# A Winograd-style convolution kernel: fewer matmuls on zeros, loads in another order, one product moved

## The chip, the cores and the metric

The kernel runs on one core of a Trainium2 chip. The core has a matmul engine (PE, with its weight loads shown as PEld), a vector engine (DVE), a scalar engine (ACT), a general engine (POOL) and a sync engine (SP) that here only issues DMAs. ACT and POOL can issue DMAs too. Sixteen DMA engines serve all of them. The metric is the device time of one execution in microseconds; it is a little longer than the span in the profile, which runs from the first to the last instruction.

## The reference

A one-dimensional convolution with three taps over two sequences, then a batch normalisation with given statistics, then SiLU. B = 2 sequences of S = 2048 positions, C = 1024 channels in and out, bf16 inputs:

```python
xp = jnp.pad(x, ((0, 0), (P, P), (0, 0)))
y = sum(jnp.einsum('bsc,cd->bsd', xp[:, k:k + S, :], w[k]) for k in range(K))
inv_std = 1.0 / jnp.sqrt(var + 1e-5)
y = (y - mean) * (g * inv_std) + b
return _silu(y)
```

## The kernel before

**The method.** Six neighbouring outputs are made from eight inputs by eight products (numbered 0 to 7, one for each evaluation point) instead of eighteen. There are 342 groups of six outputs in each sequence.

**Input transform.** For each sequence `bi` and each of the 8 channel tiles `ct`, a load (`load_x`, 512 KB) brings 16 frames of 128 positions. One matmul per frame with the fixed matrix `rm` (168 columns, line 292) makes the transformed input in PSUM; six or four such matmuls share a pair of PSUM banks and are one job (`Jobs.do`). ACT or DVE copies the pair to the bf16 tile `T_sb` (lines 306 and 308). The last 6 groups of a sequence come from a short block `xl` (`load_small`, 8 matmuls of 48 columns, line 281). In the text, x(b,ct) is the tile `ct` of sequence b. Tiles of x have six buffers, so the seventh load waits until PE has used the first.

**Weight transform.** For each output tile `dc` POOL, with help from ACT (line 144) and DVE (line 160), makes six transformed weight tiles `u` from the three taps (lines 146 to 167). Products 0 and 7 use taps 0 and 2 as they are. Before that POOL computes the normalisation's scale and shift from the parameters `prm` (lines 236 to 243).

**Units.** A unit is one output tile of one sequence: 8 products of 8 accumulating matmuls of 342 columns each. The first unit is a class of its own (`First`, line 462), the other fourteen and the two halves of the last one use `Unit.run` (line 336). ACT and DVE combine the products and ACT applies SiLU. In `Unit.run` the products come in the order 1, 3, 2, 4, 5, 6. Product 5 goes to bank 2 of the unit's four, ACT copies it out, and product 6 is then added in the same bank; so product 6 waits for that copy. In later units, work of the unit before stands between 5 and 6 (`behind(5)`); in the second unit there is none.

**What sets the order.** The kernel writes the order of every engine's instructions out by hand, as the program is built. For the first part it keeps a small plan: `clock` holds a planned time for each engine and for the DMA stream, `landed` the planned landing of each load, and each job is given to the PSUM bank pair that is planned to be free first and to ACT or DVE, whichever is planned to end first. While sequence 0 is transformed, `keep_busy` puts matmuls on a tile of zeros (line 101) wherever the plan sees PE waiting. They write to the bank that the next job will use. Then the main loop takes turns between sequence 1's jobs and the first unit's products, whichever the plan has ready. From the second unit on no plan is used.

**Queues.** SP issues nearly all loads, in program order: short block 0, the first halves of x(0,0) and x(0,1), x(0,2), taps 0 and 2, x(0,3) to x(0,5), tap 1, x(0,6), x(0,7), short block 1, and sequence 1's tiles. ACT issues `rm` and the two second halves. POOL issues `prm`. Loads on SP's and ACT's queues take one of eight landing semaphores in turn, so a load waits until the load eight places before it has landed.

Of the kernel before, what the change touches and what calls it, by code (L numbers as in the profile page):

```python
# [9 lines left out]
FP32 = mybir.dt.float32  # L10
BF16 = mybir.dt.bfloat16
ENG = mybir.EngineType

P = 128
# [2 lines left out]
WT = 21  # L17
XBUFS = 6
WARM_AT = 7000.0
LROWS = 48  # L20
NTILES = 342
NBP = 384
# [3 lines left out]
def kernel(  # L26
# [9 lines left out]
    nc = tc.nc  # L36
    B, CT, _, NF, _ = x.shape
    DC = w.shape[0]
# [5 lines left out]
    consts = ctx.enter_context(tc.tile_pool(name="consts", bufs=1))  # L44
# [17 lines left out]
    ps = pspool.tile([P, 8, 512], FP32, name="ps")  # L62
# [3 lines left out]
    rm = consts.tile([P, NJ, WT], BF16, name="rm")  # L66
    nc.scalar.dma_start(out=rm, in_=rm_in)
    prm = consts.tile([P, 4, DC], BF16, name="prm")
    nc.gpsimd.dma_start(out=prm, in_=prm_in)

    zeros = consts.tile([P, 384], BF16, name="zeros")
    nc.vector.memset(zeros, 0.0)
    dummy = consts.tile([P, 2], FP32, name="dummy")
    nc.vector.memset(dummy, 0.0)


    clock = {"pe": 1150.0, "act": 3700.0, "dve": 1500.0, "pool": 7000.0, "dma": 2300.0}
    cost = {"act": (0.833, 170.0), "dve": (1.042, 155.0), "pool": (2.0, 80.0)}

    def ends(e, size, ready):  # L80
# [2 lines left out]
    def busy(e, size, ready=None):  # L83
        clock[e] = ends(e, size, clock["pe"] + 250.0 if ready is None else ready)
        return clock[e] + 100.0
# [8 lines left out]
    def matmuls(cols):  # L94
        clock["pe"] += cols / (2.34 if clock["pe"] > WARM_AT else 1.18)

    def keep_busy(until, bank):

        n = 384 if clock["pe"] > WARM_AT else 192
        while clock["pe"] + 150.0 < until:  # L100
            nc.tensor.matmul(ps[:, bank, 0:n], lhsT=zeros[:, 0:P], rhs=zeros[:, 0:n], start=True, stop=True)  # L101
            matmuls(n)

    xt, xt_at, raw, raw_at = {}, {}, {}, {}
    small, small_at = {}, {}
# [1 line left out]
    def load_small(bi):  # L107
        t = xlpool.tile([P, CT * P], BF16, name="xl")
        nc.sync.dma_start(out=t[0:LROWS], in_=xl[bi])  # L109
        small[bi], small_at[bi] = t, landed(LROWS * CT * P * 2)  # L110

    def load_x(bi, ct, parts=1):
        t = xpool.tile([P, NF, P], BF16, name="xw")
        xt[bi, ct], xt_at[bi, ct] = t, []
        step = NF // parts
        for q in range(parts):
            s = slice(q * step, (q + 1) * step)
            (nc.scalar if q else nc.sync).dma_start(out=t[:, s], in_=x[bi, ct, :, s])
            at = landed(P * step * P * 2)
            xt_at[bi, ct] += [at] * step  # L120

    def load_w(dc, taps):
        if dc not in raw:
            raw[dc] = wpools[dc // 2 % 2].tile([P, 3, CT, P], BF16, name=f"wch{dc // 2 % 2}")
        if len(taps) == 3:
            nc.sync.dma_start(out=raw[dc], in_=w[dc])
        else:
            for k in taps:
                nc.sync.dma_start(out=raw[dc][:, k], in_=w[dc, :, k])
        for k in taps:  # L130
            raw_at[dc, k] = landed(P * CT * P * 2)
# [117 lines left out]
    class Jobs:  # L249


        def __init__(self, bi):
            self.bi = bi
            self.todo = [(None, 0, 0)] + [
                (ct, f, min(6, NF - f)) for ct in range(CT) for f in range(0, NF, 6)
            ]

        def __bool__(self):
            return bool(self.todo)
# [60 lines left out]
    class Unit:  # L320
# [57 lines left out]
                (first, lambda: self.first(between)),  # L378
            ][::1 if first >= min(last, 5) else -1]

        def run(self, between, also=(), prepare=None, later=False):
            def behind(n):
                for at, f in also:
                    if at == n:
                        f()

            b0, b1, b2, b3 = self.bank
            sl = slice(self.lo, self.hi)
            sd = dpool.tile([P, 4, NB], FP32, name="sd")[:, 0:3:2, sl]
            t0 = dpool.tile([P, 2, NB], FP32, name="t0")[:, :, sl]  # L390
            t2 = dpool.tile([P, 2, NB], FP32, name="t2")[:, :, sl]
            self.y23 = t1 = ypool2.tile([P, 2, NB], FP32, name="t1")[:, :, sl]
            self.product(3, 1, False, between)
            pa = self.copy(3)
            behind(1)
            self.product(0, 3, False, between)
            pb = self.copy(0, by=4.0)
            behind(2)
            self.product(3, 2, True, between)
            self.copy(3, dst=sd[:, 0])  # L400
            self.combine(sd[:, 1], pa, 2.0, b3, ALU.subtract)
            behind(3)
            self.product(0, 4, True, between)
            behind(4)
            self.combine(b1, b0, -2.0, pb)
            for t, a in ((t0, -0.0125), (t1, -0.05), (t2, -0.2)):
                self.combine(t, self.low, a, sd)
            idle(dve_work)
            if prepare:
                prepare_w(prepare)  # L410
            self.product(2, 5, False, between)
            pc = self.copy(2)
            behind(5)
            self.product(2, 6, True, between)
            self.combine(b3, b2, -0.5, pc)
            self.combine(self.low, self.high, -1.6, t0)
            self.combine(t1, self.high, -0.4, t1)
            self.combine(self.high, self.high, -0.1, t2)
            behind(6)
            if prepare and not later:  # L420
                idle(act_work)
                idle(dve_work)
# [123 lines left out]

    load_small(0)
    load_x(0, 0, 2)  # L550
    load_x(0, 1, 2)
    nc.scalar.activation(dummy[:, 1:2], dummy[:, 0:1], ACT.Silu)
    for ct in range(2, CT):
        load_x(0, ct)
        if ct == 2:
            load_w(0, (0, 2))
        if ct == 5:
            load_w(0, (1,))
    load_small(1)
    for ct in range(CT):  # L560
        load_x(1, ct)
# [19 lines left out]
    while jobs[1] or unit.todo[0][0] != 6:  # L581
        if len(second) == 3 and len(jobs[1].todo) < 6:
            second.pop(0)()
        at = jobs[1].place()[1] if jobs[1] else None
        if at is not None and (not unit.todo or at <= max(clock["pe"], unit.at())):
            jobs[1].do()
        else:
            unit.do()
# [6 lines left out]
    for i, (dc, bi) in enumerate(seq[1:-1], 1):  # L595
        unit = Unit(dc, bi, i % 2 * 4)
        also = prev.rest(quiet)
        if i == 1:
            also = [(1, second[0]), (4, second[1])] + also
        if i == 2:  # L600
            also = prev.rest(quiet, 4, 5)
        if i == 3:
            also = also + [(1, lambda: idle(act_work)), (1, lambda: idle(dve_work))]
        if i == len(seq) - 2:
            also = prev.rest(quiet, 4, 5)
        unit.run(
            quiet, also,
            2 if i == 2 else dc + 2 if bi == 1 and 0 < dc < DC - 2 else None, i == 2,
        )
        if bi == 0 and dc + 3 < DC:  # L610
            load_w(dc + 3, (0, 1, 2))
        prev.store(nc.sync)
        prev = unit

    dc, bi = seq[-1]
# [87 lines left out]
```

## Time and profile before

| | |
|---|---|
| time, median of 3 runs | 185.26 us (185.02 to 186.8) |
| time of the profiled execution | 185.67 us |
| its span | 183.9 us |
| PE, DVE, ACT, POOL busy | 176.6, 149.1, 110.0, 141.6 us |
| DMA | 24.60 MB, mean 134 GB/s |
| granted TensorE clock | 1.000 |

A page of the profile names an instruction by engine and line, then what it writes and reads. The chain of waits is followed back from the last instruction: each piece is what the next one had to wait for. Matmuls overlap, so a group's busy time includes one drain; the pace is the distance between starts. The matmuls' rate is best read from that pace, since the row of the granted clock shows full speed in every slice.

### The profile page before, as it was taken

How to read it: one execution, taken by the hardware profiler on the slowest of the kernel's cores; microseconds unless marked ns; L12 is line 12 of the kernel's file. 1: busy time of each engine (PE TensorE's matmuls, PEld its weight loads, DVE VectorE, ACT ScalarE, POOL GpSimd, SP SyncE). 2: the span in 40 equal slices, each digit the busy share in tenths (PEclk: the TensorE clock that was granted, in tenths of full speed). 3: DMA queues.
4: the chain of work that ended last, by engine and by line, in shares of the span. 5: the costliest groups of instructions: out<-in, count | busy, mean ns of one | idle time of the engine just before them, and what ended most of it. 6: DMA issues, size and time to landing. Idle time of an engine off the chain costs nothing.

```text
span 183.9 us, 3516 instructions
## 1 busy us (share of the span) xinstructions
PE 176.6 (96%) x1385; PEld 127.1 (69%) x1385; DVE 149.1 (81%) x192; ACT 110.0 (60%) x174; POOL 141.6 (77%) x78
## 2 busy tenths in 40 slices
PE   6999999898999999999999999999999999999992
PEld 4988888765666666666666666666666666668891
DVE  1169768699977999999997899789978999766690
ACT  3688997945665565456554745474547454563763
POOL 3599999989996779999999999999999776000000
PEclk9999999999999999999999999999999999999999
DMA  5999991080307030363036303620202020113042
GB/s 177 400 418 371 411 384 68 16 303 29 130 0 267 36 128 4 76 225 128 4 76 223 128 4 56 243 112 18 110 22 96 32 94 40 79 49 129 3 176 86
DMA packets 7089, 24.60 MB, mean 134 GB/s; under 512 B 944, under 2 KB 1344, under 8 KB 7072
## 3 DMA queue, kind: packets, MB, share of 16 engines
q1 hardware_dynamic: 6464, 23.73, 35.2%
q10 hardware_dynamic: 576, 0.63, 1.0%
q8 instruction: 11, 0.18, 0.4%
q14 instruction: 6, 0.05, 0.1%
q0 software_dynamic: 32, 0.01, 0.1%
HBM read 14.93 MB, written 9.44 MB: 132 GB/s over the span
## 4 chain that ended last, share of the span: by engine, by line
PE 89%; DVE 4%; ACT 3%; DMA 2%; issue 1%; SPq 0%; DVEq 0%; ACTq 0%
PE ps L336 73%; PE ps L292 10%; PE ps L462 4%; DMA xw<-in_x_dram 2%; DVE ps L352 2%; PE ps L101 1%; DVE T_sb L308 1%; ACT T_sb L306 1%; DVE t L352 1%; ACT yh L357 1%; ACT w1x L144 1%; ACT pc L345 0%; SPq L109 0%; DVEq L692 0%; PE ps L281 0%
## 5 line engine op out<-in xcount | busy, mean ns | idle before, releaser
L336 PE MATMUL ps<-T_sb,u 128*128 128x342 bf16 (+2 forms) x768 | 109.8, 298 | 0.5 <-ACT pc L345 0.5
L336 PEld LDWEIGHTS <-u 128*128 128x128 bf16 x768 | 72.5, 97 | 33.4 <-issue 0.7
L167 POOL TENSOR_TENSOR u<-e,w1x 128x1024 bf16<-128x1024 f32 x32 | 69.3, 2193 | 7.1 <-DVE e L160 6.4
L336 PE MATMUL ps<-T_sb,wch 128*128 128x342 bf16 (+2 forms) x256 | 39.8, 299 | 0.2 <-DVE ps L352 0.2
L167 POOL TENSOR_TENSOR u<-e,wch 128x1024 bf16<-128x1024 f32 x16 | 37.6, 2369 | 0.6
L352 DVE SCALAR_TENSOR_TENSOR t<-ps,sd 128x684 f32<-128x684 f32 (+2 forms) x49 | 37.5, 819 | 0.6
L357 ACT ACTIVATE yT<-ps,beta,scale 128x342 bf16<-128x342 f32 (+1 forms) x42 | 29.2, 727 | 10.9 <-PE ps L336 10.9
L345 ACT COPY pc<-ps 128x342 f32<-128x342 f32 (+2 forms) x32 | 13.6, 426 | 30.6 <-PE ps L336 28.8
L336 PEld LDWEIGHTS <-wch 128*128 128x128 bf16 x256 | 24.2, 97 | 11.1 <-issue 0.5
L308 DVE CAST T_sb<-ps 128x1008 bf16<-128x1008 f32 (+2 forms) x21 | 20.8, 1011 | 13.4 <-PE ps L292 10.2
L306 ACT CAST T_sb<-ps 128x1008 bf16<-128x1008 f32 (+1 forms) x29 | 25.6, 928 | 5.6 <-PE ps L292 5.5
L352 DVE SCALAR_TENSOR_TENSOR ps<-ps,t 128x684 f32<-128x684 f32 (+2 forms) x32 | 26.5, 829 | 0.5
L292 PE MATMUL ps<-rm,xw 128*128 128x168 bf16 x256 | 24.7, 250 | 1.2 <-ACT T_sb L306 0.7
L160 DVE SCALAR_TENSOR_TENSOR e<-wch 128x1024 f32<-128x1024 bf16 x12 | 25.7, 2141 | 0.0
L292 PEld LDWEIGHTS <-xw 128*128 128x128 bf16 x256 | 21.8, 105 | 4.4 <-issue 1.5
L352 DVE SCALAR_TENSOR_TENSOR ps<-ps,pc 128x342 f32<-128x342 f32 (+2 forms) x34 | 16.9, 496 | 8.4 <-PE ps L336 5.9
L154 POOL TENSOR_TENSOR e<-wch 128x1024 f32<-128x1024 bf16 x8 | 19.0, 2370 | 1.0 <-DMA wch<-in_w_dram 1.0
L357 ACT ACTIVATE yT<-t,beta,scale 128x684 bf16<-128x684 f32 x15 | 14.4, 958 | 0.0
L352 DVE SCALAR_TENSOR_TENSOR t<-ps,t 128x684 f32<-128x684 f32 (+2 forms) x17 | 13.9, 817 | 0.0
L352 DVE SCALAR_TENSOR_TENSOR sd<-pc,ps 128x342 f32<-128x342 f32 (+2 forms) x17 | 8.2, 483 | 6.1 <-ACT sd L345 6.1
L345 ACT COPY sd<-ps 128x342 f32<-128x342 f32 (+2 forms) x16 | 6.8, 428 | 10.4 <-PE ps L336 9.7
L347 ACT ACTIVATE pc<-ps 128x342 f32<-128x342 f32 (+2 forms) x16 | 7.0, 438 | 9.2 <-PE ps L336 6.9
(41 smaller groups left out, 69.1 us busy)
## 6 DMA issues: line engine op xcount, KB each, us to landing
out_dram<-yT SPq DMA_DIRECT2D x15, 576.0 KB, 2.7
xw<-in_x_dram SPq DMA_DIRECT2D x14, 512.0 KB, 6.7
wch<-in_w_dram SPq DMA_DIRECT2D x7, 768.0 KB, 5.4
wch<-in_w_dram SPq DMA_DIRECT2D x3, 256.0 KB, 6.1
xw<-in_x_dram ACTq DMA_DIRECT2D x2, 256.0 KB, 4.6
xw<-in_x_dram SPq DMA_DIRECT2D x2, 256.0 KB, 4.5
out_dram<-yh SPq DMA_DIRECT2D x1, 256.0 KB, 3.7
out_dram<-yh SPq DMA_DIRECT2D x2, 128.0 KB, 2.1
```

Source lines behind the costliest of these rows:

```text
L154: nc.gpsimd.tensor_tensor(sums[dc, q], a, b, op=ALU.add)
L160: nc.vector.scalar_tensor_tensor(out=e, in0=f, scalar=4.0, in1=h, op0=ALU.mult, op1=ALU.add)
L167: nc.gpsimd.tensor_tensor(wts[dc, q][:, i], sums[dc, q], o, op=(ALU.add, ALU.subtract)[i])
L292: nc.tensor.matmul(src[:, q // per, q % per], lhsT=xt[self.bi, ct][:, f + q], rhs=rm, start=True, stop=True)
L306: nc.scalar.copy(dst, src)
L308: nc.vector.tensor_copy(dst, src)
L336: nc.tensor.matmul(self.bank[q], lhsT=lhsT, rhs=T_sb[self.bi][:, ct, j, nsl], start=not add and ct == 0, stop=ct == CT - 1, skip_group_che ...
L345: nc.scalar.copy(dst, self.bank[q])
L347: nc.scalar.mul(dst, self.bank[q], by)
L352: nc.vector.scalar_tensor_tensor(out=out, in0=in0, scalar=scalar, in1=in1, op0=ALU.mult, op1=op1)
L357: nc.scalar.activation(self.yT[:, rows, self.y0:self.y0 + self.hi - self.lo], src, ACT.Silu, bias=beta[:, dc:dc + 1], scale=scale[:, dc:dc ...
L462: nc.tensor.matmul(self.bank[q], lhsT=lhsT, rhs=T_sb[self.bi][:, ct, j, :], start=not add and ct == 0, stop=ct == CT - 1, skip_group_check ...
```

## The change

Zeros: the tile of zeros becomes fp32 with 256 columns, three fp32 matmuls on it are issued ahead of everything, and `keep_busy` works (on the same bytes, read as bf16) only where the plan sees a longer wait: over 200 ns before a planned 9 us, over 900 ns after. In the built program 25 matmuls on zeros become three fp32 ones and five of 192 columns; none of 384 columns are left.

Loads: x(0,0) and x(0,1) come first and the short block third on SP's queue; tap 1 comes behind all of sequence 0's tiles (sequence 1 in the change's own words, which count from one). The parameters go from POOL's queue to ACT's, behind the second halves of x(0,0) and x(0,1).

Jobs: each sequence's short block becomes the seventh job instead of the first. The plan also books 0.85 us plus overhead on ACT when one of the second tile's weight steps is put on ACT. In the new order of PE, sequence 0's tiles 2 to 7 and the first 12 matmuls of x(1,0) follow each other with nothing between, and the first unit's products begin after that.

Second unit: product 5 and the copy behind it come ahead of product 4 (`early`).

```diff
+FILL = 9000.0
@@
-    nc.gpsimd.dma_start(out=prm, in_=prm_in)
-
-    zeros = consts.tile([P, 384], BF16, name="zeros")
+
+    zeros = consts.tile([P, 256], FP32, name="zeros")
     nc.vector.memset(zeros, 0.0)
+    for _ in range(3):
+        nc.tensor.matmul(ps[:, 3, 0:256], lhsT=zeros[:, 0:P], rhs=zeros, start=True, stop=True)
@@
-    clock = {"pe": 1150.0, "act": 3700.0, "dve": 1500.0, "pool": 7000.0, "dma": 2300.0}
+    clock = {"pe": 4150.0, "act": 3700.0, "dve": 1500.0, "pool": 7000.0, "dma": 2300.0}
@@ def keep_busy(until, bank):
-        n = 384 if clock["pe"] > WARM_AT else 192
-        while clock["pe"] + 150.0 < until:
-            nc.tensor.matmul(ps[:, bank, 0:n], lhsT=zeros[:, 0:P], rhs=zeros[:, 0:n], start=True, stop=True)
-            matmuls(n)
+        z = zeros.bitcast(BF16)
+        n, gap, left = (192, 200.0, 100.0) if clock["pe"] < FILL else (384, 900.0, 600.0)
+        if clock["pe"] + gap < until:
+            while clock["pe"] + left < until:
+                nc.tensor.matmul(ps[:, bank, 0:n], lhsT=z[:, 0:P], rhs=z[:, 0:n], start=True, stop=True)
+                matmuls(n)
@@ class Jobs
-            self.todo = [(None, 0, 0)] + [
-                (ct, f, min(6, NF - f)) for ct in range(CT) for f in range(0, NF, 6)
-            ]
+            self.todo = [(ct, f, min(6, NF - f)) for ct in range(CT) for f in range(0, NF, 6)]
+            self.todo.insert(6, (None, 0, 0))
@@ Unit.run(..., early=False)
             self.combine(sd[:, 1], pa, 2.0, b3, ALU.subtract)
             behind(3)
+            if early:
+                self.product(2, 5, False, between)
+                pc = self.copy(2)
             self.product(0, 4, True, between)
             behind(4)
@@
-            self.product(2, 5, False, between)
-            pc = self.copy(2)
+            if not early:
+                self.product(2, 5, False, between)
+                pc = self.copy(2)
             behind(5)
@@
-    load_small(0)
     load_x(0, 0, 2)
     load_x(0, 1, 2)
+    load_small(0)
+    nc.scalar.dma_start(out=prm, in_=prm_in)
     nc.scalar.activation(dummy[:, 1:2], dummy[:, 0:1], ACT.Silu)
     for ct in range(2, CT):
         load_x(0, ct)
         if ct == 2:
             load_w(0, (0, 2))
-        if ct == 5:
-            load_w(0, (1,))
+    load_w(0, (1,))
     load_small(1)
@@
             second.pop(0)()
+            busy("act", CT * P, 0.0)
```

In the call of `unit.run`, `early` is true for the second unit alone (`i == 1`).

More of the change, by code (lines that the diff above doesn't have):

```diff
@@ L379, in rest, with run @@
             ][::1 if first >= min(last, 5) else -1]
-        def run(self, between, also=(), prepare=None, later=False):
+        def run(self, between, also=(), prepare=None, later=False, early=False):
             def behind(n):
@@ L607 @@
             quiet, also,
-            2 if i == 2 else dc + 2 if bi == 1 and 0 < dc < DC - 2 else None, i == 2,
+            2 if i == 2 else dc + 2 if bi == 1 and 0 < dc < DC - 2 else None, i == 2, i == 1,
         )
```

## The prediction

> **What bounds the kernel now.** I read the page first: one core, granted clock full in every slice, PE busy.
>
> ```profile
> span 183.9 us, 3516 instructions
> PE 176.6 (96%) x1385; PEld 127.1 (69%) x1385; DVE 149.1 (81%) x192; ACT 110.0 (60%) x174; POOL 141.6 (77%) x78
> ```
>
> PE bounds the average, so the chain of waits was next (start, length, what, count).
>
> ```profile
> 1.17 3.77 DMA xw<-in_x_dram
> ...
> 4.98 4.68 PE ps L292 x32
> ...
> 10.66 0.48 PE ps L101 x2
> ...
> 11.44 0.65 PE ps L101 x4
> 12.09 0.88 PE ps L292 x12
> ...
> 25.21 1.01 ACT T_sb L306
> ...
> 40.59 4.66 PE ps L336 x32
> 45.25 0.02 issue
> 45.27 0.45 ACT pc L345
> 45.73 0.04 issue
> 45.77 128.81 PE ps L336 x904
> ```
>
> From 45.77 to 174.6 PE never waits; behind that comes a tail that the change leaves alone. All that can move lies before 45.77. There the first 32 input-transform matmuls (L292) take 146 ns each and later ones 73 (12 in 0.88), and matmuls on zeros (L101) stand in the chain among useful work. Third, the same time as stretches (length, then busy time by engine, granted clock, DMA share, GB/s):
>
> ```profile
> 4.98:9.64 4.66, 4.66 (x34) 4.66 (x35) 0.86 (x1) 3.26 (x4) 2.94 (x7) 1.00 1.04 404
> 9.64:19.30 9.66, 9.41 (x108) 7.98 (x106) 8.10 (x8) 8.54 (x11) 9.36 (x7) 1.00 1.03 397
> 19.30:40.43 21.13, 20.43 (x210) 16.60 (x210) 15.84 (x20) 17.07 (x23) 21.04 (x10) 1.00 0.62 227
> 45.07:45.77 0.70, 0.17 (x3) 0.00 (x0) 0.67 (x1) 0.50 (x2) 0.70 (x2) 1.00 0.00 0
> ```
>
> Up to 19.3 us, where sequence 0's 128 transform matmuls end, the DMA engines are full at about 400 GB/s. Last, SP's timeline and the transfers issued around 11.5 us, for the first tile of sequence 1, x(1,0):
>
> ```profile
> 11.47 12.32 SPq L118 DMA_DIRECT2D xw<-in_x_dram x8
> ```
> ```profile
> xw<-in_x_dram SPq DMA_DIRECT2D x1, 512.0 KB, 7.6
> ```
>
> So x(1,0) lands at 11.47 + 7.6 = 19.1. Its first matmul is at 19.65: PE trails the loads by only 0.5 us here.
>
> **Zeros, and what they hide.** Eleven 384-column zeros go, at 163 ns each (0.65 / 4): 1.8 us of PE. Five of 192 columns stay, 0.4 us at that rate per column. This does not reach the end in full. In the new order sequence 0's 128 matmuls and the first 12 of x(1,0) run on end, and x(1,0) cannot come much earlier: the bytes ahead of its last one are the same in both orders (tap 1's 262 KB passes x(0,6) and x(0,7), not x(1,0)). These are nine x tiles of 524 KB, three weight taps of 262, two short blocks of 98 and 51 of parameters, 5.75 MB. At 241 GB/s over 1 to 5 us and 400 after, they are read by 17.0; landing takes until 19.1. I take 19.1. PE then waits for it instead of working on zeros.
>
> From x(1,0) on, PE needs 128 x 73 ns for sequence 1, 64 products of the first unit (`First`) and 8 of the second at 145 ns (4.66 / 32): 9.3 + 9.3 + 1.2 = 19.8 us, whatever the order. Before, this ran from 19.65 to 40.43, 20.8 us, so 1.0 was lost; two waits for a PSUM bank, 25.9 to 26.3 and 34.05 to 34.76, are nearly all of it. The second stands behind ACT's 1.06 us w1x (L144) in the middle of the copies; the change books that time in the plan. After, PE starts at 19.15 and also has sequence 1's short block behind x(1,0), 8 matmuls in 0.3 us. I walked the new order down, job by job: a job of 6 (or 4) matmuls starts when PE is free, its tile has landed and the copy out of its bank pair has ended; its copy starts 0.28 us after its last matmul or when its engine is free, with the trace's pitch (ACT 0.90 us for 1008 columns, 0.61 for 672; DVE 1.17 and 0.82). Over the old order this gives 40.4, as the trace has. Over the new one sequence 0 keeps up with its loads (last tile taken at 16.7, last matmul at 17.8), PE waits until 19.15, and later there are two bank waits, 0.24 and 0.20, both at x(1,3). So 19.15 + 19.8 + 0.3 + 0.45 = 39.7, against 40.43: **0.75 us gained.** Walked with x(1,0) at 18.2 the gain is 1.65, at 19.7 it is 0.15.
>
> **fp32 zeros at the start.** The trace has no fp32 matmul. From below: 192 bf16 columns go every 0.16 us (11 in 1.94, the last one's drain in it), so 256 columns in one pass 0.21, three 0.64. From above: ACT's 1.0 us for a copy of 1008 fp32 columns, for each, 3.0 (the plan, which starts PE's clock at 4150 instead of 1150 ns, books as much). PE starts at 1.15 (the memset of 0.22 us is a third longer); x(0,0) lands at 4.9, and about 4.3 with the short block's 98 KB no longer ahead of it on SP's queue. So 3.2 us are free, and the price is nothing at both ends. Were they 0.8 us too long, sequence 0 would begin 0.8 late and still end before 19.15. The Trainium skill ("FP8 and Floating Point Precision", TensorE Precision Notes) says a true fp32 matmul makes four passes; by that, an estimate of 0.85 each, 2.6 in all, also hidden. What they may bring is an earlier full rate. The trace has PE working from 1.11 us and halving its matmul time only at about 9.6, after pauses at 3.0 and 4.4. The Trainium skill ("TensorE: Matmul & The Clock Gate", Part 1) has the array at full rate after one busy window of some 3.4 us; the trace took longer. By the rule the new start would be fast from 6 instead of 9.6, 24 matmuls x 70 ns = 1.7 us. By my walk that is worth nothing, since PE then waits for x(1,0) so much longer. A full rate that came only at 11.3, 7 us behind x(0,0) instead of 4.7, would cost 0.45 of the gain; I keep that for the range.
>
> **Loads that move.** Each hardware-queue load waits for the landing of the one eight places before. The parameters join this ring on ACT's queue, so SP's w and x issues slip by 0.8 to 1.4 us at 2.6 to 6 us; transfers stand 6.7 us in the queue (median), which covers it. If cover failed, x(1,0) would slip as much. Tap 1 lands about 0.7 behind x(0,7) (17.5 before), so near 17.5; POOL wants it at 18.1. POOL's timeline (start, length, instruction, idle time before it and what ended that):
>
> ```profile
> 5.34 0.20 POOL L238 TENSOR_SCALAR sc<-prm 128x8 f32<-128x8 bf16 x1 [2.50 <-DMA prm<-in_prm_dram]
> ...
> 9.38 2.12 POOL L154 TENSOR_TENSOR e<-wch 128x1024 f32<-128x1024 bf16 x1 [0.97 <-DMA wch<-in_w_dram]
> ```
>
> POOL's own issue of the parameters (0.76 us) goes, at no gain, since POOL then waits 2.50 for them. On ACT's queue they follow x(0,1)'s second half (issued 1.65, landing 7.0). POOL's scale chain (5.34 to 8.41) starts near 7.1, and the POOL work queued behind it slips 0.8 us, 9.38 to 10.2. Its tightest customer is the third unit's fifth product at 52.7, whose weights were ready at 49.6: 3.1 us of slack, 1.7 after the gain. 0.6 of the slip vanishes in POOL's own wait for w1x at 41.05. Nothing; if prm lands after 8.5 it bites one for one. ACT issues it in 0.45 us before its table load, which now ends at 3.9; the first copy is at 5.4.
>
> **Product 5 ahead of product 4.** At 45.07 PE waits 0.70 us for ACT to copy the second unit's bank 2 (0.45 at 45.27) before product 6 may be added there. Now product 4, 8 x 145 = 1.16 us, stands between. The copy needs 0.35 + 0.45: hidden, **0.70 us gained**, if ACT is free. It is: the copy now goes ahead of the second w1x, which slips to end by 44.8, and POOL wants it at 45.2. DVE's combine behind product 4 stood at 44.55, after a queue of the first unit's work; now product 4 ends at 39.7 + 4 x 1.16 = 44.3, and it stands at 44.5. So DVE still leaves that bank at 48.87, and PE, which added the next product there at 51.57, comes at 50.1: free, with 1.2 left.
>
> **Sum.** 0.75 + 0.70 = 1.45 off the span, 183.9 to 182.45. The profiled execution took 185.67, 1.77 more than its span; the median of the runs is 185.26. On that: **183.8**.
>
> **Rivals.**
> *The loads land earlier* (0.20). The reading is done by 17.0 and the landing 2.1 later; if that lag is one slow DMA engine and it does not recur, x(1,0) at 18.2 gives 1.65 + 0.70, **182.9**. Against: all later tiles lag alike.
> *The product moved brings nothing* (0.17): ACT still has sequence 1's copies or w1x in front, and the wait only moves. 0.75 remains: **184.5**. Against: ACT idles 0.75 to 0.9 us before each copy there.
> *The clock falls* (0.10). PE now idles some 0.5 us at 16.2 and 1.3 at 17.8, where zeros stood. If the half rate returns as at the start, PE works 4.66 us at half rate (4.98 to 9.64) and loses 2.3: 1.45 gained becomes 0.85 lost, **186.1**; twice, 188.4. It decides once such pauses count. For it: with 0.32 and 0.54 us of idling ahead of 4.98 the rate stayed half. Against: in the tail PE is busy only 5.5 of 9.3 us and its last matmuls still run 55 ns apart for 128 columns, full rate. The Trainium skill (same page, "HAM oscillation") has the clock fall only behind pauses above some 3.4 us; by that it stays.
>
> **Numbers.** Forecast 0.53, the rivals as given. The range, 182.8 to 185.4, takes in the early landing and the moved product that brings nothing, and leaves out most of the fallen clock and little else. One per cent, about what a measurement tells from no change, is 1.85 us: 183.4 and 187.1. Faster: the early landing, and the lower edge of the forecast, 0.26; slower, half the fallen clock and mishaps of the queues that I did not see, 0.07; the rest 0.67.
>
> **What would show it.** Right: no L101 between 9 and 40 us; a PE wait for x(1,0) just before 19.1; the second unit's matmuls (L340) unbroken from 39.7 to the tail. Wrong: x(1,0)'s first matmul away from 19.15; transform matmuls at 146 ns after 12 us; a PE wait for ACT pc near 44; POOL's first e behind 11.

## The result, and the profile after

The changed kernel takes 185.11 us in the median (184.75 to 185.66), the kernel before, timed beside it, 185.56 (185.02 to 187.23): a ratio of 0.9965, 95% interval 0.9948 to 0.9982. The forecast was 183.8, and 1.45 us of gain; 0.45 came. The 183.8 had also been counted from 185.26, the median of three runs; its twenty runs here give 185.56, so 0.3 of the miss in the time itself is that starting point. The profiled execution took 185.10, 2.1 more than its span.

The page of the changed kernel, its span and the busy time of each engine:

```profile
span 183.0 us, 3476 instructions
PE 175.1 (96%) x1371; PEld 125.1 (68%) x1371; DVE 152.1 (83%) x192; ACT 108.8 (59%) x174; POOL 141.6 (77%) x77
```

PE does 1.5 us less, DVE 3.0 more with the same 192 instructions. That is the first hint: nothing was added to DVE, so its instructions must take longer. The chain of waits (start, length, what, count):

```profile
1.16 4.47 DMA xw<-in_x_dram
...
8.49 0.57 PE ps L106 x5
...
10.25 8.71 DMA xw<-in_x_dram
19.00 1.04 PE ps L296 x12
...
36.66 1.67 DVE sd L356
...
49.55 0.80 DVE ps L356
50.39 4.82 PE ps L340 x32
...
58.70 1.86 DVE e L165
...
78.88 0.80 DVE ps L356
79.71 93.97 PE ps L340 x664
```

Before, PE ran unbroken from 45.77. Now the chain leaves PE twice more, at 50.39 and 79.71, both times for DVE's combine (L356). Between them it runs through DVE instructions of 1.67 and 1.86 us. The wait for ACT's copy at 45 us is gone. PE's waits by what ended them (total, times, longest):

```profile
PE ps L296 <- DMA xw<-in_x_dram: 2.1, 3, 1.3
...
PE ps L340 <- DVE ps L356: 0.4, 2, 0.2
```

These count idle time alone; from the start of one matmul to the start of the next, less the usual 145 ns, PE loses 0.32 and 0.30 at the two places.

The start as stretches (length, then busy time by engine with counts, granted clock, DMA share, GB/s): the first is the one shown of before, the other two are the wait for x(1,0), and what follows up to the second unit's unbroken run.

```profile
4.98:9.64 4.66, 4.24 (x51) 3.77 (x49) 2.53 (x3) 3.72 (x5) 1.30 (x2) 1.00 1.05 375
17.50:19.00 1.50, 0.23 (x4) 0.02 (x2) 1.50 (x2) 0.94 (x1) 1.42 (x2) 1.00 1.03 412
19.00:39.61 20.61, 20.48 (x208) 16.49 (x209) 15.88 (x19) 15.82 (x22) 20.53 (x11) 1.00 0.63 246
```

From 4.98 to 9.64 PE starts 51 matmuls instead of 34 but the loads bring 375 GB/s instead of 404. Then PE stands 1.5 us from start to start before x(1,0), as forecast, and needs 20.61 us from there to 39.61. SP's issue of x(1,0) (and x(1,1)), and the landing time of the first:

```profile
10.25 2.14 SPq L123 DMA_DIRECT2D xw<-in_x_dram  x2
```
```profile
xw<-in_x_dram SPq DMA_DIRECT2D x1, 512.0 KB, 8.7
```

It is issued 1.2 us earlier than before and lands at 18.95, 0.15 earlier. Last, POOL, whose chain starts with the parameters:

```profile
8.26 0.20 POOL L243 TENSOR_SCALAR sc<-prm 128x8 f32<-128x8 bf16 x1 [6.70 <-DMA prm<-in_prm_dram]
...
11.37 2.12 POOL L159 TENSOR_TENSOR e<-wch 128x1024 f32<-128x1024 bf16 x1
```

The first e stands at 11.37, not at the 10.2 of the forecast, and behind the 11 that it named as a sign of being wrong.

The two profiled executions can be added up at PE's last full-size matmul before the tail, which starts at 173.52 before and 172.63 after; the tail is 10.38 in both. The second unit's run starts 0.81 earlier (39.61 for 40.42); the wait of 0.70 at 45 us is gone; a wait of 0.32 at 50.4 and one of 0.30 at 79.7 are new. 0.81 + 0.70 - 0.32 - 0.30 = 0.89, and 173.52 - 172.63 is 0.89. That is twice the gain of the medians. The span of 183.0 is among the three shortest of the kernel's twenty executions, whose median span is 183.3; for the kernel before, the profiled span is 183.9 and the median of the executions timed beside the experiments 183.7. So the experiments ask why those two waits came, and whether the 0.81 of this one execution stands for the others.

### The profile page after: what moved, and what is told of

Same layout as the page of the kernel before. It is cut to its first block, busy times and chain, and to the rows that moved or that the text cites. A ratio compares the mean times of both kernels' runs of the same rounds, so it can differ in the third digit from the quotient of the medians.

```text
span 183.0 us, 3476 instructions
## 1 busy us (share of the span) xinstructions
PE 175.1 (96%) x1371; PEld 125.1 (68%) x1371; DVE 152.1 (83%) x192; ACT 108.8 (59%) x174; POOL 141.6 (77%) x77
## 4 chain that ended last, share of the span: by engine, by line
PE 62%; DVE 24%; DMA 7%; issue 2%; ACT 2%; DVEq 0%; ACTq 0%
PE ps L340 54%; DMA xw<-in_x_dram 7%; DVE ps L356 7%; DVE t L356 6%; PE ps L296 5%; DVE e L165 5%; PE ps L470 2%; DVE T_sb L312 2%; DVE sd L356 2%; DVE f L356 2%; ACT T_sb L310 1%; ACT yh L361 1%; PE ps L106 0%; ACTq L68 0%; DVEq L701 0%
## 5 line engine op out<-in xcount | busy, mean ns | idle before, releaser
L172 POOL TENSOR_TENSOR u<-e,wch 128x1024 bf16<-128x1024 f32 x16 | 38.8, 2439 | 0.5
L356 DVE SCALAR_TENSOR_TENSOR t<-ps,sd 128x684 f32<-128x684 f32 (+2 forms) x49 | 37.5, 819 | 0.6
L312 DVE CAST T_sb<-ps 128x1008 bf16<-128x1008 f32 (+2 forms) x22 | 22.6, 1066 | 11.7 <-PE ps L296 11.6
L310 ACT CAST T_sb<-ps 128x1008 bf16<-128x1008 f32 (+1 forms) x28 | 24.1, 892 | 5.5 <-PE ps L296 5.1
L356 DVE SCALAR_TENSOR_TENSOR ps<-ps,t 128x684 f32<-128x684 f32 (+2 forms) x32 | 26.5, 829 | 0.5
L165 DVE SCALAR_TENSOR_TENSOR e<-wch 128x1024 f32<-128x1024 bf16 x12 | 26.8, 2237 | 0.0
L296 PE MATMUL ps<-rm,xw 128*128 128x168 bf16 x256 | 23.4, 243 | 2.6 <-DMA xw<-in_x_dram 2.1
L296 PEld LDWEIGHTS <-xw 128*128 128x128 bf16 x256 | 20.2, 100 | 6.0 <-DMA xw<-in_x_dram 3.5
L356 DVE SCALAR_TENSOR_TENSOR ps<-ps,pc 128x342 f32<-128x342 f32 (+2 forms) x34 | 16.8, 495 | 8.5 <-PE ps L340 6.1
L356 DVE SCALAR_TENSOR_TENSOR t<-ps,t 128x684 f32<-128x684 f32 (+2 forms) x17 | 13.9, 817 | 0.0
L356 DVE SCALAR_TENSOR_TENSOR sd<-pc,ps 128x342 f32<-128x342 f32 (+2 forms) x17 | 8.2, 483 | 4.5 <-ACT sd L349 4.4
```

The lines of the kernel that those rows point to most:

```text
L165: nc.vector.scalar_tensor_tensor(out=e, in0=f, scalar=4.0, in1=h, op0=ALU.mult, op1=ALU.add)
L172: nc.gpsimd.tensor_tensor(wts[dc, q][:, i], sums[dc, q], o, op=(ALU.add, ALU.subtract)[i])
L296: nc.tensor.matmul(src[:, q // per, q % per], lhsT=xt[self.bi, ct][:, f + q], rhs=rm, start=True, stop=True)
L310: nc.scalar.copy(dst, src)
L312: nc.vector.tensor_copy(dst, src)
L356: nc.vector.scalar_tensor_tensor(out=out, in0=in0, scalar=scalar, in1=in1, op0=ALU.mult, op1=op1)
```

## The experiments

Seven kernels (e1 to e7) undo or single out parts of the change, e8 is the changed kernel again, and seven more (e9 to e15) test what these left open. Each was timed beside the kernel before on the same chip (medians there 185.43 to 185.56); the profiled numbers are of one execution each. "Wait at 50" and "at 80" are what PE loses there, beyond the 145 ns from one matmul to the next.

| run | median us (runs) | ratio to before, 95% | x(1,0) landed | 2nd unit's run from | DVE sd<-sd,kept, ns | wait at 45 / 50 / 80, us |
|---|---|---|---|---|---|---|
| before | 185.56 (20) | 1 | 19.10 | 40.42 | 674 | 0.70 / 0 / 0 |
| after | 185.11 (20) | 0.9965 (0.9948 to 0.9982) | 18.96 | 39.61 | 1669 | 0 / 0.32 / 0.30 |
| e1 | 185.25 (12) | 0.9983 (0.9950 to 1.0015) | 18.92 | 40.14 | 2487 | 0 / 1.41 / 0 |
| e2 | 185.60 (12) | 1.0012 (0.9983 to 1.0042) | 19.61 | 40.27 | 1764 | 0.70 / 0 / 0 |
| e3 | 185.10 (12) | 0.9968 (0.9936 to 1.0000) | 19.69 | 40.35 | 1300 | 0 / 0.32 / 0 |
| e4 | 186.12 (12) | 1.0025 (0.9990 to 1.0061) | 20.91 | 41.57 | 1274 | 0 / 0.33 / 0 |
| e5 | 185.00 (12) | 0.9972 (0.9957 to 0.9988) | 18.40 | 39.51 | 2029 | 0 / 0.66 / 0.34 |
| e6 | 185.11 (12) | 0.9975 (0.9954 to 0.9996) | 18.93 | 39.59 | 1835 | 0 / 0.47 / 0.33 |
| e7 | 185.54 (12) | 0.9998 (0.9982 to 1.0014) | 19.45 | 40.49 | none | 0 / 0.32 / 0 |
| e9 | 185.12 (12) | 0.9968 (0.9950 to 0.9986) | 19.53 | 40.20 | 1593 | 0 / 0.23 / 0.32 |
| e10 | 184.75 (12) | 0.9950 (0.9927 to 0.9972) | 19.23 | 39.90 | 1332 | 0 / 0 / 0 |
| e11 | 185.13 (12) | 0.9983 (0.9957 to 1.0009) | 18.19 | 41.49 | 2396 | 0.70 / 0 / 0 |
| e12 | 183.92 (6) | 0.9901 (0.9873 to 0.9930) | 17.80 | 38.91 | 798 | 0 / 0 / 0 |
| e13 | 184.24 (8) | 0.9937 (0.9916 to 0.9959) | 17.74 | 39.56 | 2257 | 0 / 0.89 / 0 |
| e14 | 184.67 (6) | 0.9952 (0.9935 to 0.9970) | 18.98 | 40.21 | 829 | 0 / 0 / 0 |
| e15 | 184.11 (6) | 0.9929 (0.9905 to 0.9952) | 18.05 | 39.55 | 515 | 0 / 0 / 0 |

**e1: the kernel before with the moved product alone.**

```diff
+            if early:
+                self.product(2, 5, False, between)
+                pc = self.copy(2)
             self.product(0, 4, True, between)
...
-            self.product(2, 5, False, between)
-            pc = self.copy(2)
+            if not early:
+                self.product(2, 5, False, between)
+                pc = self.copy(2)
```

> The kernel before with product 5 ahead of product 4 in the second unit and nothing else. Theory (VectorE's chain of combines and weight sums between 36 and 80 us caps what PE can gain, because those of its instructions that read two SBUF tiles wait until GpSimd's running instruction ends): PE's wait of 0.70 us at 45.1 goes, VectorE leaves bank 0 at about 48.9 while PE comes at 50.9, the first weight sum of VectorE (line 160, near 58.7) still meets an idle GpSimd and takes 1.2 us, and the chain keeps its lead at 79: the whole 0.7 us reaches the end, span about 183.2 where the kernel before has 183.9, ratio about 0.996. Rival (the moved product only moves the wait, or the gain is lost in PE's own stream): span 183.9, ratio 1.000.

The wait at 45 us goes and the median falls by 0.3, not by 0.7; the interval of its ratio takes in no change. DVE's timeline in e1 (start, length, instruction), and the chain's last long piece:

```profile
37.48 2.49 DVE L352 SCALAR_TENSOR_TENSOR sd<-sd,kept 128x342 f32<-128x342 f32 x1
...
51.08 0.87 DVE L352 SCALAR_TENSOR_TENSOR ps<-ps,t 128x684 f32<-128x684 f32 x1
```
```profile
52.00 122.99 PE ps L336 x864
```

PE now waits at 52.00 for the combine that ends at 51.95. One DVE instruction of the first unit took 2.49 us in this execution, where the kernel before shows 0.67 and the same kind of instruction on 342 columns elsewhere 0.5.

**e2: the changed kernel with the old order of products**, so zeros and loads alone.

```diff
-            2 if i == 2 else dc + 2 if bi == 1 and 0 < dc < DC - 2 else None, i == 2, i == 1,
+            2 if i == 2 else dc + 2 if bi == 1 and 0 < dc < DC - 2 else None, i == 2, False,
```

> The changed kernel with the second unit's products in the old order. Theory of VectorE's chain: PE again waits 0.70 us near 44.3, but then reaches product 0 at about 50.7, after VectorE's end at 50.3, and comes to 79.8, after VectorE's 79.7, so neither of the two new waits (0.32 and 0.30 us) is there: span about 183.1, within 0.15 us of the changed kernel. Rival (the moved product is worth its 0.7 us in the changed kernel and the loss came from elsewhere, such as the fewer zeros or the clock): 0.6 to 0.7 us slower than the changed kernel, about 183.65.

Zeros and loads alone bring nothing that can be measured. The chain of e2 shows where:

```profile
11.06 8.55 DMA xw<-in_x_dram
...
40.43 4.66 PE ps L340 x32
45.12 0.45 ACT pc L349
45.61 128.90 PE ps L340 x904
```

x(1,0), loaded by the very same instructions as in the changed kernel, lands at 19.61 here. Its first matmul is then at 19.66, where the kernel before, with all its zeros, has 19.65.

**e3 and e4: the parameters elsewhere.** e3 issues them on POOL's queue as before; in e4 the added line is `nc.scalar.dma_start`, on ACT's queue right behind rm and ahead of x.

```diff
     prm = consts.tile([P, 4, DC], BF16, name="prm")
+    nc.gpsimd.dma_start(out=prm, in_=prm_in)
...
-    nc.scalar.dma_start(out=prm, in_=prm_in)
```

> The changed kernel with the parameters loaded from GpSimd's queue again, as before. Theory of VectorE's chain: the parameters land near 5.3 us instead of 8.2, GpSimd's first weight sum starts near 9.4 instead of 11.4 and all its work stands 2 us earlier; its second tile's first pair of weights ends near 57.5 instead of 59.5, so VectorE's first weight sum near 58.6 runs alone (1.2 us instead of 1.95), the chain to 79.7 ends 0.7 earlier and PE's wait of 0.30 at 79.7 goes. The wait at 50.4 stays, since the sum of sd and kept near 36.7 still meets a running GpSimd instruction (they are 2.1 us long and the shift is 2.0). Span about 182.7, 0.3 below the changed kernel. Rival (GpSimd's lateness is hidden): no difference, 183.0.

> The changed kernel with the parameters on ScalarE's queue, but directly behind rm and ahead of the second halves of x(0,0) and x(0,1). Theory of VectorE's chain: they land near 4.5, GpSimd starts on the weights when the taps land, near 9.4, and it goes as with GpSimd's own queue: span about 182.7. x(0,0)'s second half may land up to 0.3 later, which is covered. Rival (what counts is the parameters' being on a hardware queue, in the ring of eight, or GpSimd's lateness is hidden): no difference to the changed kernel, 183.0.

With POOL's first e back at 9.64 (e3) or at 10.47 (e4) the wait at 80 is gone, and the one at 50 stays at 0.32. e3's time is that of the changed kernel all the same; in its profiled execution x(1,0) landed at 19.69. e4 is slower than the changed kernel, with x(1,0) at 20.91.

**e5 and e6: x(1,0) ahead of tap 1 and the second short block (e5); the first short block first again (e6).**

```diff
+    load_x(1, 0)
     load_w(0, (1,))
     load_small(1)
-    for ct in range(CT):
+    for ct in range(1, CT):
         load_x(1, ct)
```
```diff
+    load_small(0)
     load_x(0, 0, 2)
     load_x(0, 1, 2)
-    load_small(0)
```

> The changed kernel with x(1,0) loaded ahead of tap 1 and of sequence 1's short block; the orders of all engines but SP are the same. Theory A: x(1,0) lands 0.9 us earlier (360 KB fewer ahead of it at 400 GB/s), near 18.3, and PE's first matmul on it moves with it; then x(1,1), whose landing is unchanged, binds, so 0.45 us is left at the second unit's run, and the median is 0.3 to 0.45 below the changed kernel. Rival (the landing is hidden, or VectorE's chain takes all that PE gains): no difference.

> The changed kernel with sequence 0's short block at the head of SP's queue again, ahead of x(0,0); the orders of all other engines are the same. Theory A with the short block's place as the cause of the later stream: rm lands near 3.3 instead of 4.0, the next loads are issued earlier, the bytes up to x(1,0) are read by 17.2 instead of 17.7, x(1,0) lands at 19.0 to 19.2, and the median is 0.3 to 0.5 below the changed kernel. Rival (the stream is late because taps and x wait in the ring of eight behind one load more, or because tap 1 has moved): x(1,0) at 19.6 as in the other kernels of the new order, no difference.

e5 is the telling one. x(1,0) lands half a microsecond earlier than in the changed kernel, and PE's last full-size matmul comes at 172.90, 0.27 later: the waits at 50 and 80 grow from 0.62 to 1.00. PE's lead is given back to DVE. e6 fits neither of its theories: x(1,0) landed at 18.93, close to theory A's 19.0, but the median is the changed kernel's.

**e7: the slow DVE instruction without its second SBUF operand**, at the price of one more DVE instruction ahead of it.

```diff
+                if j == 1:
+                    nc.vector.scalar_tensor_tensor(
+                        out=self.kept[:, 1], in0=b1, scalar=2.0, in1=self.kept[:, 1], op0=ALU.mult, op1=ALU.add
+                    )
...
-                self.combine(sd[:, 3], sd[:, 2], 1.0, self.kept[:, 1])
+                self.combine(sd[:, 3], b1, -1.0, self.kept[:, 1])
```

> The changed kernel with the first unit's sum of sd and kept, which reads two SBUF tiles, made from PSUM and one SBUF tile instead; one more VectorE instruction of the same kind stands earlier, where the first product on that bank is copied. Theory B (VectorE's instructions with two SBUF inputs wait until GpSimd's running instruction ends, and behind them VectorE's unbroken chain makes PE wait): the sum takes 0.5 us instead of 1.3 to 1.7 (2.5 once), VectorE leaves bank 0 about 1 us earlier and PE's wait of 0.3 us (1.4 once) at 50 to 52 us is gone; the median is 0.3 below the changed kernel, and the spread of the runs smaller. Rival (the wait there comes from the order of the products): the wait stays, no difference.

> The changed kernel once more, unchanged, beside the three that follow. Theory A (in the new order PE waits for x(1,0), so its landing sets the end; the load stream of the new order is later than in the old one): the first matmul on x(1,0) lies between 19.0 and 19.8 us, and from there to the second unit's unbroken run it is 20.6 us again; median near 185.1. Rival (the landing is hidden and the end is set by PE's own work from x(0,0)): that distance changes by as much as the landing does.

The instruction takes 506 ns with one operand from PSUM, and the long one is gone. The added one costs as much elsewhere (PE waits at 32.4 us, and from x(1,0)'s first matmul to the second unit's run it needs 20.99 us, where the changed kernel needs 20.61), and e7 is no faster than before. The changed kernel, run once more as e8, gave 185.12 in the median of twelve runs (0.9980, 0.9958 to 1.0001); the thirteenth, its profiled execution, took 187.75 and is taken up in the last section. What e7 shows is the wait at 50, the same 0.32 though DVE is early. DVE's timeline and PE's chain in e7:

```profile
45.34 0.52 DVE L356 SCALAR_TENSOR_TENSOR ps<-ps,pc 128x342 f32<-128x342 f32 x1 [1.02 <-PE ps L340]
...
50.35 0.87 DVE L356 SCALAR_TENSOR_TENSOR ps<-ps,t 128x684 f32<-128x684 f32 x1
```
```profile
40.65 4.66 PE ps L340 x32
51.27 123.00 PE ps L340 x864
```

DVE is idle for 1.02 us, until product 4 (the last of the 32 matmuls) ends. From there it needs 5.88 us, 45.34 to 51.22, and PE, whose unbroken run starts at 40.49, wants the bank 72 matmuls later, at 40.49 + 72 x 0.145 = 50.9. So there are two ways to this wait: product 4's later place, worth 0.32 at least, and DVE's queue where the long instruction has delayed it.

**e9: product 4 back in its place; the third unit's first product between products 5 and 6.** It (`ahead.start`, the third unit's product(3, 1) and its copy) covers ACT's copy as product 4 did, and the number of matmuls ahead of each later use of a bank is the same.

```diff
-            if early:
-                self.product(2, 5, False, between)
-                pc = self.copy(2)
             self.product(0, 4, True, between)
...
+            self.product(2, 5, False, between)
+            pc = self.copy(2)
             behind(5)
+            if ahead:
+                ahead.start(between)
             self.product(2, 6, True, between)
```

> The changed kernel, but in the second unit product 4 goes back ahead of product 5, and the third unit's first product (8 matmuls) stands between products 5 and 6 and covers ACT's copy in place of product 4. The number of matmuls ahead of each later use of a bank stays the same, from the second unit's end on. Theory A (product 4's place): DVE needs some 6.1 us from the end of product 4 to the end of its last combine of the second unit, which frees PSUM bank 3 for the product 72 matmuls later; with product 4 moved 1.16 us back, the wait near 50.4 us (0.32 us in the changed kernel, the same in four variants) vanishes, except where DVE's sd<-sd,kept takes over 1.5 us: then 0 to 0.3 us are left. No wait at 45 us either. Time 0.3 us under the changed kernel, 184.8. Theory B (DVE's queue): the first unit's work on DVE, with its waits for POOL, sets when the bank is free; product 4's place does not matter: the wait near 50.4 stays at 0.3 us or more and the time at 185.1.

The wait at 50 falls to 0.23, within theory A's 0 to 0.3 for a long instruction of 1593 ns, but the time is theory B's 185.1: with POOL late, as here, DVE's queue decides. e9 also shows that the wait at 80 goes with POOL and not with a late PE: its second unit's run starts nearly as late as e3's (40.20 for 40.35), and the wait is still there.

**e10 and e12: e9, with the parameters on POOL's queue and the first short block first again; e12 also loads x(1,0) ahead of tap 1.** The loads of e12:

```diff
+    nc.gpsimd.dma_start(out=prm, in_=prm_in)
...
+    load_small(0)
     load_x(0, 0, 2)
     load_x(0, 1, 2)
-    load_small(0)
-    nc.scalar.dma_start(out=prm, in_=prm_in)
...
+    load_x(1, 0)
     load_w(0, (1,))
     load_small(1)
-    for ct in range(CT):
+    for ct in range(1, CT):
         load_x(1, ct)
```

> As the run before (third unit's first product between products 5 and 6), and with the short block of sequence 0 first on SP's queue and the parameters on POOL's queue again, as in the kernel before. Theory A: POOL's first e starts near 9.5 again, so that DVE's first e near 59 us runs alone in 1.21 us and the wait near 79.7 is gone; x(1,0) lands at 18.9 to 19.1 and its first matmul is at 19.0 to 19.1; no waits at 45, 50 and 80: last full matmul 0.6 to 0.7 us ahead of the changed kernel's 172.6, span 182.3 to 182.6, time 184.4. Theory B: DVE is full from 36 to 80 us, so that what PE gains is taken back in waits for DVE at 50 and 80 us: time 184.9 to 185.1.

> As the second run of these, and x(1,0) loaded ahead of tap 1 and of sequence 1's short block. x(1,0) lands near 18.4 to 18.6, x(1,1) then binds for 0.4 us, second unit's matmuls from 39.3 to 39.6. Theory A: no waits at 45, 50 and 80 us, span 182.2 to 182.5, time 184.2 to 184.4, faster than every kernel so far. Theory B (DVE full from 36 to 80 us): the waits at 50 and 80 come back with 0.3 to 0.6 us together, time 184.9 to 185.0, as with x(1,0) early alone.

All three waits are gone in both. The chains end in one piece, e10's and then e12's:

```profile
40.06 133.28 PE ps L341 x936
```
```profile
39.07 133.28 PE ps L341 x936
```

e10's median is 0.35 above theory A's. The profiled execution took theory A's 184.4 with x(1,0) at 19.23, so that landing does not explain the 0.35, and nothing here does. e12, at 183.92, has the lowest median of the study. In its profiled execution, the fastest of its six (183.46), x(1,0) lands at 17.80, the second unit's run starts at 38.91, and nothing of that is given back. Theory B, by which DVE is full from 36 to 80 us, has fallen: part of DVE's busy time there was waiting for POOL, and in e12 DVE even stands idle for 0.3 us ahead of product 6's combine.

**e11: the kernel before with the change of the zeros alone.**

> The kernel before with the change of the zeros alone (three fp32 ones at the start, fewer gaps filled, the plan's PE clock from 4150), loads and products as before. Theory A (the loads of the new order are what is late): x(1,0) lands at 18.9 to 19.1 as in the kernel before, PE takes it at once (first matmul at 19.0 to 19.2, not 19.65), the second unit's matmuls start 0.4 to 0.6 earlier than 40.42, the 0.70 us wait at 45 stays: span 183.4, time 185.1. Theory B (PE's work behind x(1,0), or DVE, takes back what the zeros leave): the start of the second unit's matmuls stays within 0.2 of 40.4 and the time at 185.5.

This one left the question open. The plan, whose PE clock starts later, put the transform matmuls and the first unit's products in another order, and in the profiled execution, the slowest of its twelve, the long DVE instruction (2396 ns) stood ahead of a T_sb copy that PE needed. The median gain of 0.3 is within its interval.

**e13, e14, e15: the parts seen apart.** e13 is e12 with the change's order of products. e14 is the kernel before with the third unit's product between 5 and 6 and nothing else. e15 is e12 with the old zeros and the old start of the plan.

> The fastest kernel so far (x(1,0) ahead of tap 1, parameters on POOL's queue, third unit's first product between products 5 and 6), but with the second unit in the order of the change again: product 5 ahead of product 4. Theory A (product 4's place): PE waits near 49.5 us, 0.3 us (469 ns from start to start), although DVE is early, and everything behind it is 0.3 us later: time 184.2. Theory B (DVE's queue): where DVE is early (sd<-sd,kept under 1 us) product 4's place costs nothing: no wait, time 183.9.

> The kernel before with one edit: the third unit's first product between products 5 and 6 of the second unit; zeros, loads and the parameters as before. Theory A: the 0.70 us wait at 45 us is gone and no new one comes at 51 or 80, since product 4 stays where it was: last full matmul 0.7 us ahead of 173.5, time 184.8, against 185.25 for product 5 ahead of product 4 alone. Theory B (DVE takes it back): waits of 0.3 us or more for DVE at 51 or 80 us, time 185.1 to 185.3.

> The fastest kernel so far with the zeros of the kernel before: bf16 ones at the start and in every gap, the plan's PE clock from 1150. Theory A (the zeros delay useful matmuls once x(1,0) lands early): x(1,0) still lands near 17.8 to 18.5, but PE comes to it only at 19 or later, second unit's matmuls from 39.8 to 40.4, time 184.8 to 185.2. Theory B (the gain is the loads' alone, the zeros only fill time in which PE waits anyway): first matmul of x(1,0) within 0.3 of its landing, time 183.9 to 184.2.

e13 is 0.32 slower than e12, theory A's number; since the intervals of the two ratios overlap, the timing alone does not carry it. In its profiled execution the wait is 0.89, because the long instruction took 2257 ns; and PE, at half rate until 9.2 us, took x(1,0) at 18.56, 0.82 behind its landing, where e12's took it at 17.85. e14, one edit on the kernel before, gains 0.85 at a ratio of 0.9952, no wait left at 45, 50 or 80. e15 is e14 with x(1,0) ahead of tap 1, tap 1 behind sequence 0's tiles, the short blocks as the seventh jobs and the booking on ACT. Together these bring 0.56 (184.11 for 184.67), and the old zeros cost 0.19 against e12; the intervals separate neither. In e15's profiled execution PE, at half rate until 9.8 us, took x(1,0) 0.83 behind its landing.

## Why the forecast was wrong

**The copy is hidden: right, its price wrong.** The wait at 45 us went, as forecast (0.70). What failed is the sentence "So DVE still leaves that bank at 48.87, and PE, which added the next product there at 51.57, comes at 50.1: free, with 1.2 left". The timeline of DVE in the kernel before:

```profile
47.99 0.88 DVE L352 SCALAR_TENSOR_TENSOR ps<-ps,t 128x684 f32<-128x684 f32 x1
48.77 0.86 DVE L352 SCALAR_TENSOR_TENSOR t<-ps,t 128x684 f32<-128x684 f32 x1
49.55 0.87 DVE L352 SCALAR_TENSOR_TENSOR ps<-ps,t 128x684 f32<-128x684 f32 x1
```

The first of these is the combine into the low pair of banks, which ends at 48.87. The product at 51.57 is the second unit's point at infinity, added to bank 3, in the high pair: it waits for the third, which ends at 50.42. PE coming at 50.1 is 0.3 late by these rows, not 1.2 early. The slack was read off the wrong line, and the changed kernel lost 0.32 at just that place, with DVE early (e7) or late.

**"I take 19.1": mis-sized.** The walk itself held: the second unit's run was to start 39.7 - 19.15 = 20.55 us behind x(1,0)'s first matmul and started 20.61 behind it in the changed kernel, in e2, e3 and e4. But of four profiled executions with these loads and this order up to there, x(1,0) landed at 18.96 in one and at 19.61, 19.45 and 19.53 in the others (e2, e7, e9). The forecast priced that itself: 0.15 of gain at 19.7. The profile of after shown above has the earliest of the four, and part of its 0.81 is luck; e2 started the second unit's run only 0.15 ahead of the kernel before (40.27 for 40.42). How much is luck is not shown, since the landing is known for profiled executions alone: e2's took its kernel's median time, e9's 0.5 more than its kernel's. The step that failed is "transfers stand 6.7 us in the queue (median), which covers it". SP's fourth x tile was issued at 5.64 instead of 3.71, and the rate of the loads from 3 to 5 and 5 to 7 us fell; the kernel before, then after:

```profile
3.00:5.00 2.00, 1.14 (x13) 0.75 (x13) 0.56 (x1) 0.61 (x2) 0.00 (x0) 1.00 1.04 364
5.00:7.00 2.00, 2.00 (x15) 2.00 (x16) 0.00 (x0) 0.96 (x2) 1.57 (x2) 1.00 1.04 392
```
```profile
3.00:5.00 2.00, 2.00 (x11) 1.38 (x9) 0.00 (x0) 1.09 (x2) 0.00 (x0) 1.00 1.02 342
5.00:7.00 2.00, 1.62 (x14) 1.33 (x12) 0.00 (x0) 1.55 (x2) 0.00 (x0) 1.00 1.04 346
```

The last number of each line is GB/s: (364 - 342) x 2 + (392 - 346) x 2 = 136 KB not moved, 0.34 us at 400 GB/s. It takes both small loads back in their old places to undo this. Over the first 10 us the loads run at 299 GB/s in the kernel before, at 287 in the changed kernel and at 276 to 279 in e2, e7 and e9; with the parameters alone back in their place (e3) it is 280, with the short block alone (e6) 288, and with both (e10, e12, e13) 298 to 299, and x(0,3) is issued at 3.6 to 3.7 again. That accounts for 0.3 to 0.6 us of bytes, but not for the landing: e10, with the old rate, still has x(1,0) at 19.23. "The bytes ahead of its last one are the same in both orders" was true, and was the hint that was not taken: e5, e12, e13 and e15, which take tap 1 and a short block from ahead of x(1,0), have it at 17.7 to 18.4.

**"Nothing; if prm lands after 8.5 it bites one for one": wrong.** The parameters landed at 8.18 instead of 7.0, and it bit without reaching 8.5. POOL's first e was 2.0 us later than before, and the customer that I named (the third unit's fifth product) was not the one that paid. It was DVE's own first e. Its row in the kernel before, then in the changed one:

```profile
59.39 1.21 DVE L160 SCALAR_TENSOR_TENSOR e<-wch 128x1024 f32<-128x1024 bf16 x1
```
```profile
58.60 1.95 DVE L165 SCALAR_TENSOR_TENSOR e<-wch 128x1024 f32<-128x1024 bf16 x1
```

Before, POOL had ended an instruction at 58.04 and was idle. After, it was in one until 59.47, and DVE's ended 1.08 behind that. The wait at 80 goes with it: where this e takes 1.95 to 2.01 us (after, e5, e6, e9) the wait is 0.30 to 0.34, and where it takes 1.21 to 1.68 (before and all others) there is none.

**The rest.** The three fp32 zeros took 0.85 us each and kept PE busy from 1.17 to 4.10. x(0,0)'s first half landed at 3.80 and its first matmul came at 4.01, some 0.2 behind; that cost nothing, since PE waits for the loads again from 5.29 to 5.67. The estimate by the Trainium skill ("FP8 and Floating Point Precision", TensorE Precision Notes), 0.85, agrees with this trace. The last slow transform matmul started at 6.62, close to the 6 that the Trainium skill's rule gave ("TensorE: Matmul & The Clock Gate", Part 1); with the same zeros it was 9.28 in e9 and 9.21 in e13, and in e12 none was slow, so it is not dependable. The clock did not fall over the 1.5 us pause (it reads 1.00 in the two rows from 17.50 on); in another execution it did (last section). No zeros were left between 9.06 and 40 us, as forecast.

In the profiled execution, then, the start brought 0.81 for the forecast's 0.75, the copy brought 0.70 and gave back 0.32, and the late parameters took 0.30: 0.89 of 1.45. The medians of the spans, 183.3 for 183.7, leave 0.4. The rest is this one pair of executions, the kernel before 0.2 above its median and the changed one 0.3 below. That later landings of x(1,0) are what makes the others longer fits e2, e7 and e9, but is not shown.

## What to carry to other kernels

When a product is moved to cover a wait, follow each engine's work behind the product that gave way, to the bank it frees, by the operand (which pair of banks) and not by the next row that looks alike. Cover a wait with work that nobody waits for yet: on the kernel before, the third unit's first product brought 0.85 us (e14) where the second unit's own product 4 brought 0.3 (e1), though the intervals of the two overlap. With POOL late it brought nothing over product 4 (e9, 185.12 for 185.11). And a landing time from one execution is one draw: price a step at the values that it takes over several, above all where the change takes away the filler that hid them.

## What the runs showed of the hardware

A DVE instruction with both tensors in SBUF waits for a POOL instruction that is running. In the changed kernel, DVE's and POOL's rows:

```profile
36.66 1.67 DVE L356 SCALAR_TENSOR_TENSOR sd<-sd,kept 128x342 f32<-128x342 f32 x1
```
```profile
35.83 4.49 POOL L172 TENSOR_TENSOR u<-e,wch 128x1024 bf16<-128x1024 f32 x2
```

The first of POOL's two ends at 37.96 and DVE's at 38.33. That distance is 370 to 374 ns in every execution of the table but e15 (441 ns, where the instruction took 515) and e7, which has no such instruction, and 1079 to 1089 ns for e where it had to wait, so the instruction's length (0.5 to 2.5 us) is set by where POOL happens to be. The Trainium skill states the lock ("SBUF — State Buffer", Who interferes with whom: a VectorE instruction with two SBUF inputs contends with a GpSimd instruction that reads SBUF, and the second to issue blocks); the trace agrees, and e7, with one operand in PSUM, took 506 ns. What was not expected is that a 2 us shift of POOL, by a load of 8 KB landing 1.2 us later than reckoned, changes DVE's time 50 us later.

The landing of x(1,0), 512 KB at the end of the same 5.75 MB of loads, varied by 0.65 us between executions that differ in nothing ahead of it (after, e2, e7 and e9). With the loads of the kernel before it came at 18.92 to 19.10 in three executions and at 18.19 in e11, which differs from them in its zeros and the order that the plan makes of them. Why was not found.

The rival "the clock falls" did occur. In e8's profiled execution x(1,0) landed at 20.48, PE stood for 2.18 us before it, and the granted clock (the third number from the end) reads half behind it:

```profile
20.50:23.00 2.50, 2.48 (x15) 2.11 (x16) 0.58 (x1) 1.00 (x1) 2.50 (x2) 0.50 1.02 408
```

e4's profiled execution, with 1.66 us of standing, kept 1.00. A mean granted clock below 0.99 stands in none of the 112 executions of the kernel before timed beside the experiments and in none of the changed kernel's first twenty, but in one of e8's thirteen, two of e2's, one each of e3's and e6's, and four of e4's twelve. All of these have the changed order, in which PE stands before x(1,0); e5, e7, e9, e10, e12 and e13 have it too and show none. That the standing is the cause is not shown: no run changes it alone.
